# A block-decay attention with two MLPs: a denser opening, other places for the MLP units, and weight loads on ScalarE's DMA queue

## The chip, the cores and the metric

The kernel runs on one core of a Trainium2 chip. The metric is device time in microseconds (us). Before the change three runs gave 595.54 us as their median, from 594.19 to 596.04. Engines are named as the profile names them: PE is TensorE (PEld its weight loads), DVE VectorE, ACT ScalarE, POOL GpSimd, SP SyncE.

## The reference, cut to what matters

Attention with a decay per head over 2 batches, 8 heads, 768 positions, head size 64, and then two MLPs on 1536 tokens of width 512 (inner widths 1536 and 2048), all in float32:

```python
for b in range(nb):                                   # blocks of a sequence
    intra = einsum('bhic,bhjc->bhij', qb, kb) * Dmask # lam ** (i - j), lower triangle
    intra = einsum('bhij,bhjd->bhid', intra, vb)
    inter = einsum('bhid,bhde->bhie', qb * lam_pow, kv_state)
    out[:, :, sl] = intra + inter
    kv_state = lam_block * kv_state + einsum('bhsd,bhse->bhde', kb * rev_pow, vb)
x = out as [tokens, heads * head size]
x = (silu(x @ w_gate) * (x @ w_val)) @ w_out          # first MLP
h = x @ w_in2
y = (h * cos(h)) @ w_out2                             # second MLP
```

## The kernel before

**Stages.** The attention is cut into 12 chunks g of 128 positions (6 per batch). For a chunk PE does: `t` (L1008), four transposes of q and four of k; `s` (L1025), the products of k and q; `st` (L1032), the update of the state from v and the decayed k; `av` (L1038), scores by v; `qs` (L1047), the old state by the decayed q. Between them ACT copies the transposed q and k out of PSUM (tiles qt, kt), DVE multiplies the scores with the decay mask (tile at), POOL makes the decayed k and q (kd, qd) and the decayed state (stmp), and ACT and DVE split the chunk's output into a high and a low part (xh, xl). The MLPs follow: every product is done as three fp32r matmuls of 512 columns (L140 to L142), and DVE and ACT do the activations. A weight piece comes as raw words (512 KB: one DMA of that size, or two of 256 KB for gate and val), goes through ACT (L179), DVE and ACT again, and lies in a ring as a high and a low half (wh, wl).

**Units in the attention.** Some products of the first MLP, 12 matmuls of 512 columns each ("a unit"), can run as soon as four chunks are done and their weights are there. `FILL` says after which chunk's place in the list of steps how many units stand.

**The opening.** `tables()` builds the decay mask: lam goes through a tiny matmul (L238) to all partitions, small copies put it into `powers` and `lrow`, a chain of 14 DVE instructions (L255) builds the skewed table from powers, POOL fills `lrow`, and a step `mask` (L1016) spreads the table by matmuls. In between PE multiplies a tile of zeros (`zero()`, L220), which computes nothing that is used.

**What sets the order.** A planner, run when the program is built, holds a clock per engine and hands out the instructions in the order in which they could start by its own estimates (`ATT_NS`, `free_at`, `LATENCY`, `LANDING`); each engine then runs its own list in order. Where the planner expects PE to stand idle for longer than `ZERO_FROM` before an attention step, it writes in so many zero matmuls (`COLD` or `ZERO` ns each). Every DMA before the change but one stands in SP's list (lam's is in ACT's): q, k and v by `qkv_job` (L870, one DMA of 256 KB each), weights by `load_piece` (L158 to L168). q and k have three buffers each, v five, raw weights three. In the program the DMAs take eight semaphores in turn, so each DMA waits on its queue's engine until the DMA eight before it has landed.

Of the kernel before, what the change touches and what calls it, by code (L numbers as in the profile page):

```python
# [12 lines left out]
AF = mybir.ActivationFunctionType  # L13
# [13 lines left out]
SBUFS = (6, 3)  # L27
UNIT_BANKS = 2, 4
LOOK = 4
ZERO, ZERO_FROM = 230, 300  # L30
COLD, COLD_TO = 430, 6500
KEPT = 4
TAIL = 2
SEQ = 1
# [10 lines left out]
LATENCY = 130  # L45
ISSUE = 620
LANDING = 1900
ATT_NS = {"t": 480, "mask": 700, "s": 1100, "st": 530, "av": 1080, "qs": 600}
FILL = (0, 0, 0, 0, 0, 1, 1, 1, 1, 1, 1, 1)
HELD = 6, 7, 8, 9  # L50
BUFS = {"q": 3, "k": 3, "v": 5, "qt": 2, "kt": 2, "qd": 3, "kd": 2, "at": 2, "stmp": 2}
WARM = 3, 5


FIRST = ("gate", "val", "sa", "sb", "mid")
# [3 lines left out]
def kernel(  # L59
# [19 lines left out]
    nc = tc.nc  # L79
    B, H, S, D = q.shape  # L80
    P = 128
# [3 lines left out]
    C = P  # L85
    NPAIR = H // 2
# [46 lines left out]
    def bank_tile(i):  # L133

        return banks.tile([P, 512], F32, tag=f"bank{i}", name=f"bank{i}")
# [9 lines left out]
    up_w = {"gate": w_gate, "val": w_val, "in2": w_in2}  # L145
    down_w = {"mid": w_mid, "out2": w_out2}

    raw, scaled, fp, wsp = {}, {}, {}, {}

    def load_piece(key, i):  # L150

        nm, f = key
        t = raw[key] = stage_tile(i)
        if nm in ("gate", "val"):


            for c in range(2):
                nc.sync.dma_start(  # L158
                    t[64 * c:64 * c + 64].rearrange("p (k f) -> p k f", k=KD),
                    up_w[nm][256 * c:256 * c + 256, f * 2 * P:(f + 1) * 2 * P].rearrange("(k p) f -> p k f", p=D),  # L160
                )
        elif nm in up_w:
            nc.sync.dma_start(
                t.rearrange("p (c f) -> p c f", c=KD),
                up_w[nm][:, f * 2 * P:(f + 1) * 2 * P].rearrange("(c p) f -> p c f", p=P),
            )
        else:
            nc.sync.dma_start(t, down_w[nm][f * P:(f + 1) * P, :])  # L168

    def word_tile(i):  # L170

# [25 lines left out]
    att = att_stack.enter_context(tc.tile_pool(name="att", bufs=1))  # L197
# [4 lines left out]
    lams = att.tile([1, H], F32, name="lams")  # L202
    ones = att.tile([1, P], F32, name="ones")
    powers = att.tile([P, 7, 2], F32, name="powers")
    anti = att.tile([P, P], F32, name="anti")
    dmask = att.tile([P, H, C], F32, name="dmask")
    zeros = att.tile([P, 512], mybir.dt.bfloat16, name="zeros")
    QB = 32
    skewed = [s_tile(i, f"skewed{i}")[:, 0:2 * (2 * C - QB)].rearrange("p (g y) -> p g y", g=2) for i in range(2)]
    lrow = att.tile([P, NPAIR, C], F32, name="lrow")  # L210
# [6 lines left out]

    def zero(ps, n):
        for _ in range(n):
            nc.tensor.matmul(ps, zeros[:, 0:P], zeros, start=True, stop=True)  # L220

    def tables():

        nc.vector.memset(ones, 1.0)
        nc.scalar.dma_start(lams, lam.rearrange("(o h) -> o h", o=1))
        nc.scalar.activation(warm, halfpi, AF.Silu)
        for t in skewed:
            nc.vector.memset(t, 0.0)  # L230
        for r in range(P // QB):
            nc.vector.tensor_copy(
                skewed[0][QB * r:QB * r + QB, :, C - QB:C],
                anti[QB * r:QB * r + QB, C - QB * (r + 1):C - QB * r].rearrange("p (o y) -> p o y", o=1).to_broadcast([QB, 2, QB]),
            )
        zero(bank_tile(0), WARM[0])
        every = bank_tile(1)[:, 0:H]
        nc.tensor.matmul(every, ones, lams, start=True, stop=True)  # L238
        zero(bank_tile(0), WARM[1])
        for r in range(P // QB):  # L240
            rows = slice(QB * r, QB * r + QB)
            if r % 2:
                nc.scalar.activation(powers[rows, 0, :], every[rows, 2 * r:2 * r + 2], AF.Copy)
            else:
                nc.vector.tensor_copy(powers[rows, 0, :], every[rows, 2 * r:2 * r + 2])
        for h2 in range(2):
            rows = slice(64 * h2, 64 * h2 + 64)
            nc.scalar.activation(lrow[rows, :, C - 1], every[rows, h2::2], AF.Copy)
        for i in range(7):
            m, (src, dst) = 1 << i, (skewed[i % 2], skewed[1 - i % 2])  # L250
            if i:
                nc.gpsimd.tensor_tensor(out=powers[:, i, :], in0=powers[:, i - 1, :], in1=powers[:, i - 1, :], op=ALU.mult)  # L252
            w = max(0, C - QB + 1 - 2 * m)
            for g in range(2):
                nc.vector.scalar_tensor_tensor(  # L255
                    out=dst[:, g, w:C], in0=src[:, g, w + m:C + m], scalar=powers[:, i, g:g + 1], in1=src[:, g, w:C],
                    op0=ALU.mult, op1=ALU.add,
                )
        n = 1
        while n < C:  # L260
            nc.gpsimd.tensor_tensor(
                out=lrow[:, :, C - 2 * n:C - n], in0=lrow[:, :, C - n:C],
                in1=lrow[:, :, C - n:C - n + 1].to_broadcast([P, NPAIR, n]), op=ALU.mult,
            )
            n *= 2
# [5 lines left out]
            xs[nm, blk] = tuple(xp.tile([P, KD, TB], F32R, tag=f"{t}{blk}", name=t) for t in ("xh", "xl"))  # L271
        return xs[nm, blk]

    steps_of = [("t", "q", 0), ("t", "k", 0), ("mask",), ("s", 0), ("t", "q", 1), ("t", "k", 1), ("s", 1)]
    for g in range(NCH):
        if g % CPB != CPB - 1:
            steps_of.append(("st", g))
# [39 lines left out]
    for i in range(0, NF2, GROUP2):  # L317
        p = [[("in2", 2, i + j)] for j in range(4)]
# [20 lines left out]
    def work(op):  # L339

        if op[0] in ATT_NS:
            return ATT_NS[op[0]] / 1360
        if op[0] == "h":
# [93 lines left out]
        **{nm: [(0, i) for i in range(n)] for nm, n in BUFS.items()},  # L437
    }
    wanted = {pool: [] for pool in stock}
    free_at = {"PE": 4100, "ACT": 3300, "DVE": 5900, "POOL": 7300, "SP": 700, "port": 0}  # L440
    waiting = {e: [] for e in ("ACT", "DVE", "POOL", "SP")}
    n_jobs = [0]
    pe_att, pe_units, pe_downs = [], [], []
# [46 lines left out]
    def signal(name, t):  # L490

        when[name] = t
        for job in blocked.pop(name, ()):
            resume(job, t)
# [11 lines left out]
    def go(engine, ns, fn, port=False):  # L506

        return engine, ns, fn, port or engine == "POOL"
# [25 lines left out]
    def run_all():  # L534

        while True:
            best = None
            for e in waiting:
                for job, req in waiting[e]:
                    if not allowed(e, job, req):  # L540
                        continue
                    start = max(free_at[e], job.t, free_at["port"] if req[3] else 0)
                    rank = max(start, free_at[e]), job.prio, job.n
                    if best is None or rank < best[0]:
                        best = rank, e, job, req
            op = next_pe()
            if op and (best is None or op[0] < best[0][0]):
                start, sub = op
                idle = start - free_at["PE"]
                free_at["PE"] = start + sub["ns"]  # L550
                run_pe(sub, free_at["PE"], int(idle // (COLD if start < COLD_TO else ZERO)) if pe_att and idle > ZERO_FROM else 0)
                continue
            if best is None:
                assert not pe_att and not pe_units and not pe_downs and not blocked, (pe_att[:1], pe_units[:1], pe_downs[:1], blocked, wanted)
                return
            (start, _, _), e, job, req = best
            ns = req[1]
            if req[0] == "any":
                ns = ns[e]
                waiting["DVE"].remove((job, req))  # L560
                waiting["POOL"].remove((job, req))
                req[2](e)
            else:
                waiting[e].remove((job, req))
                req[2]()
            free_at[e] = start + ns
            if req[3]:
                free_at["port"] = start + ns
            resume(job, start + ns + LATENCY)
# [58 lines left out]

    def load_job(key):

        i = yield "take", "stage"
        stage_of[key] = i
        yield from fetch(key, i)

    def fetch(key, i):

        yield go("SP", 2300 if key[0] in up_w else 1700, lambda: load_piece(key, i))
        signal(("load", key), (yield "now",) + LANDING)  # L640

    drafts = {}

# [219 lines left out]
    def qkv_job(nm, g):  # L863

        src = {"q": q, "k": k, "v": v}[nm]
        i = yield "take", nm
        t = att_tile(nm, i)
        b, c = divmod(g, CPB)
        made_att[nm, g] = i, t
        yield go("SP", 1200, lambda: nc.sync.dma_start(t, src[b, :, c * C:(c + 1) * C, :].rearrange("h p d -> p h d")))  # L870
        signal((nm, g), (yield "now",) + LANDING)

    def mask_job(got):

# [598 lines left out]
    with tc.manual_schedule():  # L1473
# [5 lines left out]
        )  # L1479
        make_identity(nc, ident)  # L1480
        tables()
        signal("skewed", 5900)
        signal("lrow", 7500)
        pe_att.extend(att_sub(op) for op in steps_of if op)
        pe_units.extend((product_sub if op[0] in ("q", "r", "h") else up_sub)(op) for op in units)
        for op in downs:
# [47 lines left out]
```

## Time and profile before

| what | value |
|---|---|
| median of three runs | 595.54 us (594.19 to 596.04) |
| the profiled execution's own time | 594.82 us |
| its span, first to last instruction | 593.0 us |
| PE busy | 586.6 us (99%) |
| DVE busy | 498.3 us (84%) |
| ACT busy | 356.4 us (60%) |
| POOL busy | 36.1 us (6%), all of it in the first 80 us |

The profile is of one execution. Its span leaves out what lies before the first and after the last instruction (594.82 against 593.0 us). The attention takes the first 79 us, then the MLPs run to the end. The times in timelines are counted from the start of the span; matmuls are pipelined, so what one kind of step costs is read from the start of its first matmul to the start of the next step's.

### The profile page before, as it was taken

Reading aid. Unit: us, or ns where it says so; the run is one execution under the profiler, and the core shown is the slowest. Engines: PE = TensorE matmul, PEld = TensorE weight load, DVE = VectorE, ACT = ScalarE, POOL = GpSimd, SP = SyncE. Lnnn points to the kernel's source line nnn. Section 1 sums busy time; section 2 is a strip of 40 time slices with the busy share of each in tenths; the row PEclk is TensorE's granted clock in tenths of the full one; section 3 lists DMA queues with packets and bytes.
Section 4 is the critical chain, followed back from the end, with each engine's and each line's share of the span. In section 5 each row is a group of like instructions: output and inputs, shape, how many; then the busy total and the mean of one; then the engine's idle time right before and its main releaser. Section 6 shows DMA issues by size and latency. Waiting matters only on the chain.

```text
span 593.0 us, 9131 instructions
## 1 busy us (share of the span) xinstructions
PE 586.6 (99%) x3372; PEld 487.5 (82%) x3372; DVE 498.3 (84%) x922; ACT 356.4 (60%) x664; POOL 36.1 (6%) x50
## 2 busy tenths in 40 slices
PE   9999999999999999999999999999999999999997
PEld 5878788888888888888888888888888888888886
DVE  5669769986699899886899999897797999998854
ACT  3664357685567556545543687977556576676620
POOL 5635200000000000000000000000000000000000
PEclk9999999999999999999999999999999999999999
DMA  9999704264576747524442433011111213100005
GB/s 191 185 204 199 157 30 107 72 202 157 162 225 198 181 141 216 159 82 162 139 161 72 143 106 106 2 55 53 55 35 56 70 54 92 51 1 0 1 6 207
DMA packets 72815, 66.65 MB, mean 112 GB/s; under 512 B 40002, under 2 KB 60738, under 8 KB 72770
## 3 DMA queue, kind: packets, MB, share of 16 engines
q1 hardware_dynamic: 72768, 66.07, 41.2%
q8 instruction: 26, 0.43, 0.3%
q14 instruction: 19, 0.16, 0.1%
q10 hardware_dynamic: 2, 0.00, 0.0%
HBM read 54.00 MB, written 12.06 MB: 111 GB/s over the span
## 4 chain that ended last, share of the span: by engine, by line
PE 97%; DMA 1%; POOL 0%; ACT 0%; issue 0%; DVE 0%
PE bank L140 25%; PE bank L141 24%; PE bank L142 24%; PE bank L1367 6%; PE bank L1368 6%; PE bank L1369 6%; PE bank L1008 2%; PE bank L1025 2%; PE bank L1038 2%; DMA k<-in_k_dram 1%; PE bank L1047 1%; PE bank L1032 1%; PE bank L220 0%; POOL powers L252 0%; PE bank L1016 0%
## 5 line engine op out<-in xcount | busy, mean ns | idle before, releaser
L140 PE MATMUL bank<-xl,wh 128*128 128x512 f32 (+1 forms) x336 | 123.5, 368 | 0.0
L141 PE MATMUL bank<-xh,wh 128*128 128x512 f32 (+1 forms) x336 | 122.5, 365 | 0.0
L142 PE MATMUL bank<-xh,wl 128*128 128x512 f32 (+1 forms) x336 | 122.3, 364 | 0.0
L522 ACT ACTIVATE s<-s 128x512 f32<-128x512 f32 (+2 forms) x112 | 66.0, 592 | 50.5 <-DVE s L515 30.6
L522 ACT ACTIVATE s<-bank 128x512 f32<-128x512 f32 (+2 forms) x114 | 61.1, 538 | 50.2 <-PE bank L142 42.9
L522 ACT ACTIVATE gh<-s 128x512 fp32r<-128x512 f32 x84 | 52.7, 627 | 46.7 <-PE bank L1368 22.3
L140 PE MATMUL bank<-wl,gh 128*128 128x512 f32 (+1 forms) x194 | 75.0, 387 | 0.0
L141 PE MATMUL bank<-wh,gh 128*128 128x512 f32 (+1 forms) x194 | 75.0, 387 | 0.0
L142 PE MATMUL bank<-wh,gl 128*128 128x512 f32 (+1 forms) x194 | 75.0, 387 | 0.0
L140 PEld LDWEIGHTS bank<-xl,wh 128*128 128x128 f32 x336 | 63.3, 188 | 12.0 <-issue 0.7
L515 DVE TENSOR_TENSOR sum<-bank,sum 128x512 f32<-128x512 f32 (+1 forms) x101 | 65.4, 679 | 9.0 <-PE bank L142 7.3
L142 PEld LDWEIGHTS bank<-xh,wl 128*128 128x128 f32 x336 | 63.3, 188 | 10.3
L141 PEld LDWEIGHTS bank<-xh,wh 128*128 128x128 f32 x336 | 63.3, 188 | 10.1
L522 ACT ACTIVATE wh<-ct 128x512 fp32r<-128x512 f32 x91 | 55.3, 627 | 23.5 <-DVE ct L191 14.9
L515 DVE TENSOR_TENSOR gl<-s,gh 128x512 fp32r<-128x512 f32 x84 | 57.5, 685 | 13.7 <-ACT gh L522 13.6
L527 DVE TENSOR_TENSOR wl<-ct,wh 128x512 fp32r<-128x512 f32 x90 | 61.2, 693 | 6.7 <-ACT wh L522 6.5
L515 DVE TENSOR_TENSOR s<-bank,s 128x512 f32<-128x512 f32 (+1 forms) x84 | 49.5, 591 | 11.2 <-PE bank L142 10.6
L1368 PE MATMUL bank<-gh,wh 128*128 128x512 f32 x144 | 56.2, 391 | 0.0
L1367 PE MATMUL bank<-gh,wl 128*128 128x512 f32 x144 | 56.2, 391 | 0.0
L1369 PE MATMUL bank<-gl,wh 128*128 128x512 f32 x144 | 56.0, 389 | 0.0
L179 ACT ACTIVATE ct<-raw 128x512 f32<-128x512 f32 x68 | 44.8, 665 | 14.1 <-DMA raw<-in_moe_w_gate_dram 6.4
L191 DVE SCALAR_TENSOR_TENSOR ct<-ct,raw 128x512 int32<-128x512 int32 x68 | 46.5, 686 | 1.6 <-ACT ct L179 0.7
(145 smaller groups left out, 980.3 us busy)
## 6 DMA issues: line engine op xcount, KB each, us to landing
raw<-in_moe_w_out_dram SPq DMA_DIRECT2D x28, 512.0 KB, 3.5
raw<-in_moe_w_in_dram SPq DMA_DIRECT2D x16, 512.0 KB, 3.9
raw<-in_moe_w_gate_dram SPq DMA_DIRECT2D x24, 256.0 KB, 5.3
raw<-in_moe_w_val_dram SPq DMA_DIRECT2D x24, 256.0 KB, 4.5
draftout<-raw SPq DMA_DIRECT2D x9, 512.0 KB, 2.6
q<-in_q_dram SPq DMA_DIRECT2D x12, 256.0 KB, 5.1
k<-in_k_dram SPq DMA_DIRECT2D x12, 256.0 KB, 5.6
v<-in_v_dram SPq DMA_DIRECT2D x12, 256.0 KB, 6.1
```

The lines of the kernel that those rows point to most:

```text
L140: nc.tensor.matmul(ps, wh, xl, start=first, stop=False, **kw)
L141: nc.tensor.matmul(ps, wh, xh, start=False, stop=False, **kw)
L142: nc.tensor.matmul(ps, wl, xh, start=False, stop=last, **kw)
L179: nc.scalar.activation(t, words[:, :, 1].bitcast(F32), AF.Prelu, scale=2.0 ** -112, alpha=2.0 ** 32)
L191: nc.vector.scalar_tensor_tensor(out=w, in0=w, scalar=3, in1=lo, op0=ALU.logical_shift_left, op1=ALU.bitwise_or)
L515: engine, n * (1.18 if engine == "DVE" else 2.45), lambda: unit.tensor_tensor(out=out, in0=in0, in1=in1, op=op),
L522: return go("ACT", 40 + n * 0.94, lambda: nc.scalar.activation(out, src, fn, **kw))
L527: return "any", {"DVE": n * 1.18, "POOL": n * 2.45}, lambda e: (nc.vector if e == "DVE" else nc.gpsimd).tensor_tensor(out=out, in0=in0, in ...
L1008: nc.tensor.transpose(ps[:, p * P:(p + 1) * P], src[:, 2 * p:2 * p + 2, :].rearrange("p a d -> p (a d)"), anti if op[1] == "q" else ident,)
L1367: nc.tensor.matmul(ps, lo[:, cs], gh, start=first, stop=False)
L1368: nc.tensor.matmul(ps, hi[:, cs], gh, start=False, stop=False)
L1369: nc.tensor.matmul(ps, hi[:, cs], gl, start=False, stop=last)
```

## The change

The zero matmuls have half as many columns (256) and half the price in the planner's eyes. lam's tiny matmul becomes six, which put the values where they are wanted, so that one DVE copy and one ACT copy stand where there were two of DVE and four of ACT. One of two memsets goes from DVE to POOL. In the list of steps the second chunk's `t` stands ahead of the first `s`. `FILL` has six units in place of seven, none before the eighth place. DMAs get one account of what has landed (`landing`). And while attention steps are left, a weight's DMA stands in ACT's list, not SP's.

```diff
-ZERO, ZERO_FROM = 230, 300
-COLD, COLD_TO = 430, 6500
+ZERO, ZERO_FROM = 115, 250
+COLD, COLD_TO = 215, 7500
...
+BEHIND = 7000
+ATT_NS = {"t": 480, "mask": 400, "s": 1100, "st": 530, "av": 1080, "qs": 600}
+FILL = (0, 0, 0, 0, 0, 0, 0, 1, 1, 1, 1, 2)
...
-WARM = 3, 5
+WARM = 4, 5
...
-    def load_piece(key, i):
+    def load_piece(key, i, queue=nc.sync):
...
-                nc.sync.dma_start(
+                queue.dma_start(
                     t[64 * c:64 * c + 64].rearrange("p (k f) -> p k f", k=KD),
...
-            nc.tensor.matmul(ps, zeros[:, 0:P], zeros, start=True, stop=True)
+            nc.tensor.matmul(ps[:, 0:256], zeros[:, 0:P], zeros, start=True, stop=True)
...
-        for t in skewed:
-            nc.vector.memset(t, 0.0)
+        nc.vector.memset(skewed[0], 0.0)
+        nc.gpsimd.memset(skewed[1], 0.0)
...
         zero(bank_tile(0), WARM[0])
-        every = bank_tile(1)[:, 0:H]
-        nc.tensor.matmul(every, ones, lams, start=True, stop=True)
+        every = bank_tile(1)
+        for r in range(P // QB):
+            nc.tensor.matmul(
+                every[QB * r:QB * r + QB, 0:2], ones[:, 0:QB], lams[:, 2 * r:2 * r + 2], start=True, stop=True, tile_position=(0, QB * r)
+            )
+        for h2 in range(2):
+            nc.tensor.matmul(
+                every[64 * h2:64 * h2 + 64, 2:2 + NPAIR], ones[:, 0:64], lams[:, h2::2], start=True, stop=True, tile_position=(0, 64 * h2)
+            )
         zero(bank_tile(0), WARM[1])
...
-                nc.vector.tensor_copy(powers[rows, 0, :], every[rows, 2 * r:2 * r + 2])
...
+        nc.vector.tensor_copy(powers[:, 0, :], every[:, 0:2])
+        nc.scalar.activation(lrow[:, :, C - 1], every[:, 2:2 + NPAIR], AF.Copy)
...
-    steps_of = [("t", "q", 0), ("t", "k", 0), ("mask",), ("s", 0), ("t", "q", 1), ("t", "k", 1), ("s", 1)]
+    steps_of = [("t", "q", 0), ("t", "k", 0), ("mask",), ("t", "q", 1), ("t", "k", 1), ("s", 0), ("s", 1)]
...
-    free_at = {"PE": 4100, "ACT": 3300, "DVE": 5900, "POOL": 7300, "SP": 700, "port": 0}
+    free_at = {"PE": 3850, "ACT": 3300, "DVE": 5700, "POOL": 7200, "SP": 500, "port": 0}
...
+    landed = [2500]
+
+    def landing(soonest, ns):
+
+        landed[0] = max(soonest, landed[0] + ns)
+        free_at["SP"] = max(free_at["SP"], landed[0] - BEHIND)
+        return landed[0] + LATENCY
...
-        yield go("SP", 2300 if key[0] in up_w else 1700, lambda: load_piece(key, i))
-        signal(("load", key), (yield "now",) + LANDING)
+        if pe_att:
+            yield go("SP", 10, lambda: None)
+            yield go("ACT", 1300, lambda: load_piece(key, i, nc.scalar))
+            signal(("load", key), landing((yield "now",) - LATENCY - 1300 + 3600, 2500))
+        else:
+            yield go("SP", 2300 if key[0] in up_w else 1700, lambda: load_piece(key, i))
+            signal(("load", key), (yield "now",) + LANDING)
```

**The opening on PE.** Before, from the last matmul of the first `s` to the second `s` (L1008 is `t`, with anti for q and ident for k; L1025 is `s`):

```order
L1025 MATMUL bank_233<-qt,kt 128x128
L1008 MATMUL bank_247<-anti,q 128x128 x4
L1008 MATMUL bank_258<-ident,k 128x128 x4
L220 LDWEIGHTS zeros
L220 MATMUL bank_272<-zeros 128x512
L220 LDWEIGHTS zeros
L220 MATMUL bank_272<-zeros 128x512
L220 LDWEIGHTS zeros
L220 MATMUL bank_272<-zeros 128x512
L1025 MATMUL bank_272<-qt,kt 128x128
```

In the changed kernel, from the last matmul of the mask (L1030) on (L1022 is `t`, L1039 `s`):

```order
L1030 MATMUL bank_215<-skewed_94,ident 32x256
L1022 MATMUL bank_234<-anti,q 128x128 x4
L1022 MATMUL bank_244<-ident,k 128x128 x4
L1039 MATMUL bank_254<-qt,kt 128x128
L1039 MATMUL bank_255<-qt,kt 128x128
```

The second chunk's transposes come before both `s`, which then follow each other; no zeros stand between them, nor between the first chunk's two transposes, where one stood before.

**The queues.** SP's list before, from the load of the sixth k on:

```order
L870 DMA k<-in_k_dram 128x8x64
L158 DMA raw<-in_moe_w_gate_dram 64x4x256 x2
L870 DMA q<-in_q_dram 128x8x64
L870 DMA v<-in_v_dram 128x8x64
L870 DMA k<-in_k_dram 128x8x64
L158 DMA raw<-in_moe_w_val_dram 64x4x256 x2
```

ACT's list in the changed kernel around the first two weight pieces (L523 are copies, x and xh of a chunk's output):

```order
L159 DMA raw<-in_moe_w_gate_dram 64x4x256 x2
L523 ACTIVATE xh<-bank_535 128x2x128
L523 ACTIVATE xh<-bank_536 128x2x128
L523 ACTIVATE qt<-bank_577 128x512
L523 ACTIVATE kt<-bank_588 128x512
L523 ACTIVATE x_98<-bank_535 128x128
L523 ACTIVATE x_99<-bank_536 128x128
L523 ACTIVATE x_100<-bank_535 128x128
L523 ACTIVATE x_101<-bank_536 128x128
L159 DMA raw<-in_moe_w_val_dram 64x4x256 x2
```

Before, a pair of gate DMAs stood between the sixth and the seventh k (the first and the third L870 k row of the piece above are these two). In the changed kernel the seventh k follows only q and v, and the pair stands in ACT's list, with the copies qt and kt, on which `s` waits, behind it. In all, 16 weight DMAs are in ACT's list, and none is in SP's until the last v has been issued.

**Zeros later in the attention.** In the changed kernel, between the ninth k's transposes and the tenth q's (L221 are zeros):

```order
L1022 MATMUL bank_773<-ident,k 128x128 x4
L221 LDWEIGHTS zeros
L221 MATMUL bank_788<-zeros 128x256
L221 LDWEIGHTS zeros
L221 MATMUL bank_788<-zeros 128x256
L221 LDWEIGHTS zeros
L221 MATMUL bank_788<-zeros 128x256
L221 LDWEIGHTS zeros
L221 MATMUL bank_788<-zeros 128x256
L221 LDWEIGHTS zeros
L221 MATMUL bank_788<-zeros 128x256
L1022 MATMUL bank_788<-anti,q 128x128 x4
```

Five zeros stand here and seven a few steps earlier, ahead of the `st` of the first chunk of the second batch. Before the change two units and no zeros stood in this part of the list; now the first unit comes one `t` and one `s` after these rows.

## Rows read from the trace of the kernel before

**Rows 1.** PE's waits over the span: for whom, us in total, times, longest
```profile
PE bank L1008 <- DMA k<-in_k_dram: 1.4, 1, 1.4
```

**Rows 2.** Busy us (x instructions) by stretch: PE, PEld, DVE, ACT, POOL, PEclk, DMA, GB/s
```profile
20.00:30.00 10.00, 10.00 (x164) 8.34 (x163) 6.86 (x15) 6.20 (x19) 5.53 (x6) 1.00 0.97 186
...
80.00:589.00 509.00, 509.00 (x2439) 427.26 (x2438) 444.01 (x795) 316.91 (x565) 0.00 (x0) 1.00 0.33 101
```

**Rows 3.** Timeline of the stall: start, us, engine, line, what, [idle before <-releaser]
```profile
30.06 0.69 PE L1032 MATMUL bank<-v,kd 128*64 128x64 f32 x16
32.14 0.63 PE L1008 MATMUL bank<-ident,k 128*128 128x128 f32 x4 [1.39 <-DMA k<-in_k_dram]
```

**Rows 4.** Timeline of the opening, PE
```profile
1.19 1.46 PE L220 MATMUL bank<-zeros 128*128 128x512 bf16 x3 [1.19 <-DVE halfpi L1475]
2.58 0.59 PE L238 MATMUL bank<-lams,ones 1*128 1x8 f32 x2
3.10 2.31 PE L220 MATMUL bank<-zeros 128*128 128x512 bf16 x5
5.52 1.09 PE L1008 MATMUL bank<-anti,q 128*128 128x128 f32 x4
6.40 0.63 PE L220 MATMUL bank<-zeros 128*128 128x512 bf16 x1
6.83 1.06 PE L1008 MATMUL bank<-ident,k 128*128 128x128 f32 x4
7.82 1.16 PE L1016 MATMUL bank<-skewed,ident 32*32 32x256 f32 x32
8.90 1.35 PE L1025 MATMUL bank<-qt,kt 64*128 64x128 f32 x16
10.18 0.66 PE L1008 MATMUL bank<-anti,q 128*128 128x128 f32 x4
10.68 0.60 PE L1008 MATMUL bank<-ident,k 128*128 128x128 f32 x4
11.12 0.81 PE L220 MATMUL bank<-zeros 128*128 128x512 bf16 x3
12.02 1.16 PE L1025 MATMUL bank<-qt,kt 64*128 64x128 f32 x16
13.11 0.69 PE L1032 MATMUL bank<-v,kd 128*64 128x64 f32 x16
```

**Rows 5.** DMA from issue to landing: first q, second k, seventh k
```profile
DMA to landing us min/median/max: 3.4/3.4/3.4
...
DMA to landing us min/median/max: 4.9/4.9/4.9
...
DMA to landing us min/median/max: 7.9/7.9/7.9
```

**Rows 6.** Timeline of DMA issues (ACTq, SPq) and of the DVE chain
```profile
0.73 0.51 ACTq L227 DMA_DIRECT2D lams<-in_lam_dram  x1
0.74 0.43 SPq L870 DMA_DIRECT2D q<-in_q_dram  x1
2.86 0.93 SPq L870 DMA_DIRECT2D k<-in_k_dram  x1
3.97 2.92 DVE L255 SCALAR_TENSOR_TENSOR skewed<-skewed,powers 128x33 f32<-128x33 f32 x14 [0.23 <-ACT powers L243]
...
19.57 1.67 SPq L158 DMA_DIRECT2D raw<-in_moe_w_gate_dram  x2
24.12 3.10 SPq L870 DMA_DIRECT2D k<-in_k_dram  x1
...
69.77 1.27 SPq L158 DMA_DIRECT2D raw<-in_moe_w_gate_dram  x2
```

**Rows 7.** Groups on ACT from 13 to 40 us: shapes, count, busy, mean ns, idle
```profile
L522 ACT ACTIVATE qt<-bank 128x512 f32<-128x512 f32 x5 | 3.0, 609 | 0.3 <-PE bank L1008 0.3
```

More of the change, by code (lines that the diff above doesn't have):

```diff
@@ L47 @@
 LANDING = 1900
-ATT_NS = {"t": 480, "mask": 700, "s": 1100, "st": 530, "av": 1080, "qs": 600}
-FILL = (0, 0, 0, 0, 0, 1, 1, 1, 1, 1, 1, 1)
+BEHIND = 7000
+ATT_NS = {"t": 480, "mask": 400, "s": 1100, "st": 530, "av": 1080, "qs": 600}
+FILL = (0, 0, 0, 0, 0, 0, 0, 1, 1, 1, 1, 2)
 HELD = 6, 7, 8, 9
 BUFS = {"q": 3, "k": 3, "v": 5, "qt": 2, "kt": 2, "qd": 3, "kd": 2, "at": 2, "stmp": 2}
-WARM = 3, 5
+WARM = 4, 5
 FIRST = ("gate", "val", "sa", "sb", "mid")
@@ L162, in load_piece @@
         elif nm in up_w:
-            nc.sync.dma_start(
+            queue.dma_start(
                 t.rearrange("p (c f) -> p c f", c=KD),
@@ L167, in load_piece @@
         else:
-            nc.sync.dma_start(t, down_w[nm][f * P:(f + 1) * P, :])
+            queue.dma_start(t, down_w[nm][f * P:(f + 1) * P, :])
     def word_tile(i):
@@ L206 @@
     dmask = att.tile([P, H, C], F32, name="dmask")
-    zeros = att.tile([P, 512], mybir.dt.bfloat16, name="zeros")
+    zeros = att.tile([P, 256], mybir.dt.bfloat16, name="zeros")
     QB = 32
@@ L236, in tables @@
         zero(bank_tile(0), WARM[0])
-        every = bank_tile(1)[:, 0:H]
-        nc.tensor.matmul(every, ones, lams, start=True, stop=True)
-        zero(bank_tile(0), WARM[1])
[L240 to L244, printed above, removed]
-                nc.vector.tensor_copy(powers[rows, 0, :], every[rows, 2 * r:2 * r + 2])
-        for h2 in range(2):
-            rows = slice(64 * h2, 64 * h2 + 64)
-            nc.scalar.activation(lrow[rows, :, C - 1], every[rows, h2::2], AF.Copy)
+        every = bank_tile(1)
[7 more added lines that the diff above has]
+            )
+        zero(bank_tile(0), WARM[1])
+        nc.vector.tensor_copy(powers[:, 0, :], every[:, 0:2])
+        nc.scalar.activation(lrow[:, :, C - 1], every[:, 2:2 + NPAIR], AF.Copy)
         for i in range(7):
@@ L549, in run_all @@
                 idle = start - free_at["PE"]
-                free_at["PE"] = start + sub["ns"]
+                free_at["PE"] = start + sub["ns"] * (2 if start < COLD_TO else 1)
                 run_pe(sub, free_at["PE"], int(idle // (COLD if start < COLD_TO else ZERO)) if pe_att and idle > ZERO_FROM else 0)
@@ L869, in qkv_job @@
         made_att[nm, g] = i, t
-        yield go("SP", 1200, lambda: nc.sync.dma_start(t, src[b, :, c * C:(c + 1) * C, :].rearrange("h p d -> p h d")))
-        signal((nm, g), (yield "now",) + LANDING)
+        yield go("SP", 1100, lambda: nc.sync.dma_start(t, src[b, :, c * C:(c + 1) * C, :].rearrange("h p d -> p h d")))
+        signal((nm, g), landing((yield "now",) - LATENCY - 1100 + 3000, 1200 if landed[0] < 12000 else 1350))
     def mask_job(got):
@@ L1481 @@
         tables()
-        signal("skewed", 5900)
-        signal("lrow", 7500)
+        signal("skewed", 5750)
+        signal("lrow", 7250)
         pe_att.extend(att_sub(op) for op in steps_of if op)
```

## The prediction, made before the result was known

> **What bounds the kernel now.** I read the page's table of engines first, then PE's waits, PE's busy time by stretch, and the timelines of the two places where PE is not full: the opening and about 31 us. From 80 us to 589 us PE is busy for 509.00 of 509.00 us [rows 2], and its list of waits over the whole span has one entry of any size, 1.4 us on a k [rows 1]. So the end is PE's work plus what PE loses in its first 80 us. The change leaves the number of useful matmuls as it is (only lam's, six for one, are more), and the last ones stand in the same order. What it can move is the opening, the one wait, and the zeros. Of the page: DVE is 84% busy, so a wait for DVE later on is possible, but before the change there is none.
>
> The sum is made against the profiled execution (594.82 us, span 593.0); the median of the three runs is 0.7 above it. I carry the difference over to the median. Runs of this kernel differ by up to 1.9 us, and about 0.3% (1.8 us) is what a measurement tells from no change.
>
> **The opening, before.** Steps cost, start to start [rows 4]: a zero of 512 columns 0.43 (6.40 to 6.83), `t` of one tensor 0.88 (5.52 to 6.40) and later 0.50 (10.18 to 10.68), the mask 1.08, the first `s` 1.28, the second 1.09. So TensorE runs at its lower level (1.2 GHz) up to the first `s` and at the upper (2.4 GHz) behind it; PE had been busy nearly without a break since 1.19 us. The first `t` starts at 5.52, behind five zeros that began at 3.10 and lasted 2.31, though its q landed at 0.74 + 3.4 = 4.1 [rows 5, 6]. The second `s` ends at 13.11.
>
> **The opening, after, step by step.**
> - Zeros ahead of lam: four of half width, 4 x 0.21 for 3 x 0.43, 0.4 us less (half of 0.43 for half of the columns is an estimate).
> - lam: 2 passes took 0.52 (2.58 to 3.10); now 12. The mask's 32 passes, which also go to small places of the array, took 1.08, or 0.03 each; at 0.26 each, as before, 12 would be 3.1, at the mask's pitch 0.4. Nearer to the mask, as these too have tile positions: I take 1.0, 0.5 more.
> - Zeros behind lam: 5 x 0.21 for 5 x 0.43: 1.1 us less. So the first `t` starts at 5.52 - 0.4 + 0.5 - 1.1 = 4.5 (not before 4.1, the landing), and the zero of 0.43 behind it is gone: the second `t` starts at 5.4 and ends at 6.3.
> - The mask then waits for the DVE chain, before 3.97 to 6.89 [rows 6]. It began after copies that alternated between DVE and ACT; with one copy, lam ready about as before, it begins some 0.5 earlier and ends at 6.4. Mask 6.4 to 7.5 (before 7.82 to 8.90).
> - The second chunk's two `t`, 0.9 each, to 9.3. They need the second k, landed at 2.86 + 4.9 = 7.8; it is there in time. kt of that chunk is copied by ACT, as qt in 0.61 [rows 7], beside the first `s`.
> - Two `s` at 1.09: to 11.5, if the clock rises by then as it did before. The three zeros of 0.81 that filled the wait for kt are gone.
> Gain 13.1 - 11.5 = 1.6 us. Bounds: if the clock rises only behind both `s`, these take twice as long (+2.2): a loss of 0.6. If it rises before the second chunk's `t`, those take 0.5 each and the k's landing sets them: 7.8 + 0.5 + 2.2 = 10.5, a gain of 2.6.
>
> **The wait at 31 us.** PE waits 1.39 us for the seventh k at 32.14 [rows 3]. That k was issued at 24.12, the issue took 3.10 and it landed 7.9 us after its start, 32.0, behind a gate pair issued at 19.57 [rows 5, 6]. The pair now comes after it. The pair's own issue takes 1.67, and it has as many bytes as two k's: the k should land two landings earlier, about 30. PE asks for it at 30.7 less the opening's gain, about 29. Of 1.39 us I count 1.2 as gained, and what is late next is again data: under a faster PE the stream of q, k and v is hardly ahead. Bounds: 0 and 1.4.
>
> **The new zeros.** Twelve of 256 columns at the upper clock: half of a fast 512-column zero. Three of those span 0.81 with the last one's pipeline in it [rows 4]; at half of the cold 0.43 a wide one is 0.21, a narrow one 0.11. 12 x 0.11 = 1.3 us of PE for nothing useful, unless PE would have waited there: then they cost nothing. They stand before an `st` that needs a v and a kd, and before a q. Bounds 0 to 1.3 of loss; I take 1.0.
>
> **Units.** One unit fewer inside the attention is one more behind it, the same twelve matmuls: nothing, covered by nothing and needing no cover, as PE is busy either way.
>
> **ACT's new work.** 16 DMAs to issue. SP took 0.64 for each of a pair when nothing was queued (1.27 for two) and 0.84 when much was (1.67) [rows 6]. A pair thus holds ACT for 1.3 to 1.7 us. ACT is busy for 6.20 of 10 us at 20 to 30 us [rows 2], so 3.8 are free. A pair comes about once a chunk; twelve chunks with their seven units take 79 us, 6.6 each, and one without a unit some 5, in which 1.9 us are free: it fits, with 0.2 to 0.6 to spare. Behind a pair in ACT's list stand xh, qt and kt, and `s` waits for the last two; and each DMA of a pair waits until the DMA eight earlier has landed, in a stream where the seventh k took 7.9 us. That is near. I put 0.4 us of PE waits here; bounds 0 and, with a whole issue of 3.10 in front of each DMA, 2 x 3.7 = 7.4 a pair, 5.5 more than is free.
>
> **Sum.** -1.6 - 1.2 + 1.0 + 0.4 = -1.4 us: 593.4 against the profiled 594.82, or 594.1 at the level of the median. That is 0.24% and inside of what can be told from no change.
>
> **Rivals.**
> 1. More is gained: the clock is up before the second chunk's `t`, the wait is gone and the new zeros stand where PE would have waited: -2.6 - 1.4 + 0.2 = -3.8 at most; with half of the zeros real waits and the opening at -2.2, -2.9: 592.6. For it: nothing but useful work now stands between the first chunk and the second `s`, 1.2 us of zeros less. Against: lam's passes and the clock.
> 2. The stream gives it all back. The first `st` of the second batch then waits for its v as long as PE came earlier: the q, k, v and weights are the same bytes on the same DMA engines, and in 20 to 30 us their share is 0.97 already [rows 2]. Then only the wait's place changes: 0 to -0.4, 595.3. Against: no weights now stand before the seventh k, and after the wait at 31 us PE never waited for a DMA again.
> The Trainium skill ("DMA: Bandwidth & Descriptors", section "Issuing engines are not separate DMA queues") has a rule for this one: a DMA runs on the same 16 engines whichever engine issues it, and issuing from several saves only the issuing time. By it the second queue gives no bandwidth and the sum would be this rival's 595.3. No row here has two full queues at once, so the trace does not decide.
> 3. Slower: ACT is held by its DMA issues. While SP's list is pushing a transfer into a full queue (3.10 for the k), ACT's issue stands still, and with it qt and kt. A first sign: the tiny load of lam, issued by ACT at 0.73, took 0.51 and ended when SP's issue of 0.43 at 0.74 had [rows 6]. If each ACT issue waits out an ordinary one of 1.0, a pair takes 3.3 and overshoots the 1.9 that are free by 1.4; if a long one, by 5.5. Two pairs come while SP is still busy and no unit covers PE: +2.8 to +11; taken +4.5, 598.2. It decides from 1.9 us a pair on. Against it: by the time of the third pair SP is nearly done with q, k and v.
> The Trainium skill ("Perfetto Trace Analysis", section "DMA Instruction — HWDGE (DVE, Sync)") states that the block which writes descriptors is locked by one sequencer at a time. By that rule this rival would hold; the one overlap at 0.73 agrees with it, and no row shows it under load.
>
> **How the numbers follow.** Forecast 0.50 (own range 593.2 to 595.0), more gained 0.22, given back 0.16, slower 0.12. Below 593.75 (faster by over 0.3%) lie a third of the forecast's case and nearly all of the first rival's: 0.38. Above 597.3 lies most of the third's: 0.10. Between them 0.52. The range leaves out the lower half of the first rival and most of the third: 592.4 to 596.4.
>
> **What would show it.** Right: the second `s` ends near 11.5; the first `t` at 4.5; no wait for k near 30; twelve zeros of 0.11 with no wait just behind them; weight issues on ACT of 0.6 to 0.9 each. Wrong: `t` at 0.88 beyond 10 us or an `s` of 2 us (the clock later); waits of PE on ACT's kt or qt behind a weight issue, or issues on ACT of over 1 us (rival 3); a wait of PE on v or q behind the zeros (rival 2); any wait of PE after 80 us.

## The result: slower by 1.2%

The changed kernel took 602.70 us (median of five runs, 598.71 to 603.98), the kernel before 595.06 beside it: ratio 1.0121 [1.0095, 1.0147]. Forecast was 594.1, with a range to 596.4. The profiled execution is the shortest of the five (598.71 us, span 596.9), so the profile shows the loss at its smallest.

PE's list of waits for the changed kernel (for whom, us in total, times, longest), to be held against [rows 1]:
```profile
PE bank L1022 <- DMA k<-in_k_dram: 2.7, 2, 2.3
PE bank L1039 <- ACT kt L523: 1.3, 1, 1.3
...
PE bank L1022 <- DMA q<-in_q_dram: 0.4, 1, 0.4
```
One wait of 1.4 us on a k has become 3.1 us on q and k, and 1.3 on kt. The stretches say where (columns as in [rows 2]; the last row is the whole time behind the attention):
```profile
28.00:32.00 4.00, 4.00 (x76) 3.37 (x68) 2.22 (x5) 2.40 (x8) 0.51 (x1) 1.00 1.18 210
32.00:36.00 4.00, 1.30 (x23) 0.88 (x22) 2.44 (x6) 1.15 (x3) 0.03 (x1) 0.94 1.16 201
36.00:40.00 4.00, 4.00 (x40) 3.06 (x40) 0.49 (x2) 1.30 (x4) 2.25 (x2) 0.63 1.28 198
...
80.00:590.00 510.00, 509.89 (x2451) 428.04 (x2450) 445.85 (x793) 319.23 (x569) 0.00 (x0) 1.00 0.33 100
```
From 32 to 36 us PE works 1.30 of 4 us, and in the next four it is busy at a granted clock of 0.63. From 80 us on next to nothing is lost (0.11 us). PE's timeline there:
```profile
33.02 0.63 PE L1022 MATMUL bank<-anti,q 128*128 128x128 f32 x4 [0.39 <-DMA q<-in_q_dram]
35.95 1.09 PE L1022 MATMUL bank<-ident,k 128*128 128x128 f32 x4 [2.31 <-DMA k<-in_k_dram]
36.96 1.98 PE L1052 MATMUL bank<-at,v 128*64 128x128 f32 x16
...
41.16 0.94 PE L221 MATMUL bank<-zeros 128*128 128x256 bf16 x7
42.03 0.69 PE L1046 MATMUL bank<-v,kd 128*64 128x64 f32 x16
42.54 1.05 PE L1052 MATMUL bank<-at,v 128*64 128x128 f32 x16
```
The eighth k is late, and behind that pause an `av` takes 1.98 us instead of 1.05: TensorE is at its lower level (1.2 GHz). The seven zeros later on have no wait behind them.

The opening, against [rows 4]:
```profile
2.09 0.28 PE L240 MATMUL bank<-lams,ones 1*32 1x2 f32 x8
2.30 0.38 PE L244 MATMUL bank<-lams,ones 1*64 1x4 f32 x4
2.61 1.25 PE L221 MATMUL bank<-zeros 128*128 128x256 bf16 x5
4.35 1.08 PE L1022 MATMUL bank<-anti,q 128*128 128x128 f32 x4 [0.49 <-POOL powers L253]
...
7.66 0.91 PE L1022 MATMUL bank<-anti,q 128*128 128x128 f32 x4
...
8.93 2.25 PE L1039 MATMUL bank<-qt,kt 64*128 64x128 f32 x32
11.11 0.66 PE L1022 MATMUL bank<-anti,q 128*128 128x128 f32 x4
```
The second `s` ends at 11.11; before it ended at 13.11. The opening gained 2.0 us, and more than that was lost between 16 and 54 us. For this execution the account closes: -2.0 of the opening, +3.0 of waits (4.4 on q, k and kt for 1.4), +1.5 of half clock (0.37 of the 4 us from 36 to 40) and +1.4 of the twelve zeros (0.87 and 0.55, start to start) make the 3.9 us by which its span is longer than before.

### The profile page after: what moved, and what is told of

It reads as the page before. It is cut to its first block, busy times and chain, and to the rows that moved or that the text cites. A ratio compares the mean times of both kernels' runs of the same rounds, so it can differ in the third digit from the quotient of the medians.

```text
span 596.9 us, 9166 instructions
## 1 busy us (share of the span) xinstructions
PE 587.6 (98%) x3391; PEld 489.8 (82%) x3391; DVE 500.9 (84%) x921; ACT 356.1 (60%) x661; POOL 33.6 (6%) x50
## 4 chain that ended last, share of the span: by engine, by line
PE 90%; DMA 5%; DVE 2%; ACT 1%; POOL 1%; issue 1%; SPq 0%; ACTq 0%; DVEq 0%; POOLq 0%
PE bank L141 23%; PE bank L142 23%; PE bank L143 23%; PE bank L1381 5%; PE bank L1382 5%; PE bank L1383 5%; DMA k<-in_k_dram 3%; PE bank L1022 2%; PE bank L1052 1%; DMA q<-in_q_dram 1%; DMA raw<-in_moe_w_gate_dram 1%; PE bank L1039 1%; PE bank L1061 1%; DVE s L516 1%; DVE ct L192 1%
## 5 line engine op out<-in xcount | busy, mean ns | idle before, releaser
L523 ACT ACTIVATE s<-bank 128x512 f32<-128x512 f32 (+2 forms) x114 | 61.1, 538 | 52.1 <-PE bank L143 47.2
L523 ACT ACTIVATE gh<-s 128x512 fp32r<-128x512 f32 x84 | 52.9, 631 | 58.2 <-PE bank L1382 31.2
L523 ACT ACTIVATE s<-s 128x512 f32<-128x512 f32 (+2 forms) x112 | 65.5, 589 | 30.8 <-DVE s L516 19.2
L523 ACT ACTIVATE wh<-ct 128x512 fp32r<-128x512 f32 x91 | 55.6, 627 | 28.0 <-DVE ct L192 20.6
```

What stands on the lines that cost most here:

```text
L523: return go("ACT", 40 + n * 0.94, lambda: nc.scalar.activation(out, src, fn, **kw))
```

## The experiments

Theory A: the second queue does the harm. It has two ways: A1, weights on ScalarE's queue pass q, k and v on the transfer engines; A2, ScalarE is held by its weight issues, and kt and qt behind them. Theory B: the units, which now stand later, no longer cover the stream. Theory C: the zeros. In the diffs `-` and `+` are against the changed kernel unless another is named. Every ratio is to the kernel before, run beside it. Some expectations count from 0: the "sixth k" of two of them is the seventh k of the front, and "k of the seventh chunk" is the eighth k here.

**The queue undone.**
```
-            yield go("ACT", 1300, lambda: load_piece(key, i, nc.scalar))
+            yield go("ACT", 1300, lambda: load_piece(key, i))
```


> The changed kernel with one thing undone: the weights of the attention are issued by SyncE, at the same place of the program's order, so that q, k, v and weights come in one row; TensorE's order stays the same to the instruction. Theory A (the second queue: from 26 to 42 us the weights on ScalarE's queue take more than half of the transfer engines, q and k of the seventh chunk come late, TensorE waits 2.7 us on them, the clock goes to half for 3.4 us and a weight issue that stands on ScalarE holds kt for 1.3 us): none of the three is seen, k of the seventh chunk lands by 31 us instead of 35.8, and the time is 592 to 594.5, below before. Theory B (the later units: no MLP unit stands before the eighth chunk, so TensorE runs into data whatever queue brings it): a wait on q or k of 2 us or more stays between 30 and 40 us, the clock still falls there, and the time is 599 to 603. Theory C (the twelve new zero multiplies and the shorter opening's own costs): no data wait, but 598 or more.

594.81 us, ratio 0.9995 [0.9979, 1.0010]: the whole loss is gone, as A said, though the time lies just above A's range (592 to 594.5). PE's waits on data:
```profile
PE bank L1022 <- DMA k<-in_k_dram: 0.8, 1, 0.8
PE bank L1022 <- DMA q<-in_q_dram: 0.4, 1, 0.4
```
How the eighth k came late is seen in the two queues. The profile's rows of DMA queues from 26 to 40 us (packets, MB, share of 16 engines), the changed kernel's first, then this one's:
```profile
DMA packets 8192, 2.89 MB, mean 206 GB/s; under 512 B 7164, under 2 KB 8188, under 8 KB 8188
...
q1 hardware_dynamic: 7101, 1.79, 77.6%
q10 hardware_dynamic: 1087, 1.05, 39.0%
```
```profile
DMA packets 7915, 2.74 MB, mean 196 GB/s; under 512 B 6992, under 2 KB 7911, under 8 KB 7911
...
q1 hardware_dynamic: 7911, 2.69, 99.4%
```
The sum is nearly the same, 206 and 196 GB/s: a second queue (q10, ScalarE's) brought no bandwidth worth the name. What differs is the order. The first gate pair and the eighth k as they were issued, with two queues and then with one:
```profile
25.64 0.74 ACTq L159 DMA_DIRECT2D raw<-in_moe_w_gate_dram  x1
...
26.03 0.99 SPq L884 DMA_DIRECT2D k<-in_k_dram  x1
26.43 0.62 ACTq L159 DMA_DIRECT2D raw<-in_moe_w_gate_dram  x1
```
```profile
25.54 0.98 SPq L884 DMA_DIRECT2D k<-in_k_dram  x1
...
27.69 3.11 SPq L159 DMA_DIRECT2D raw<-in_moe_w_gate_dram  x2
```
With one queue the pair stands behind that k; with two it goes beside it, and the weights take their part (39.0% against the 77.6% of SyncE's queue; not more than half, as the expectation has it) while the k is on its way. From issue to landing the eighth k took 9.8 us with two queues and 6.2 us with one:
```profile
DMA to landing us min/median/max: 9.8/9.8/9.8
```
```profile
DMA to landing us min/median/max: 6.2/6.2/6.2
```

**The units put back.**
```
-FILL = (0, 0, 0, 0, 0, 0, 0, 1, 1, 1, 1, 2)
+FILL = (0, 0, 0, 0, 0, 1, 1, 1, 1, 1, 1, 1)
```


> The changed kernel with the units put back to where they stood before (one in each chunk from the sixth on); the weights stay on ScalarE's queue. Theory A (second queue): q, k and v still come late while weights are under way, and the unit in the sixth chunk now waits for its weights too: 598 to 603. Theory B (later units): the unit at 34 to 37 us covers the seventh k, no wait over 1 us on it, the clock stays up, 592.5 to 595. Theory C (zeros): 598 or more without data waits.

599.83 us, 1.0079 [1.0057, 1.0102]. The time is in A's range. It is 2.9 us below the changed kernel, and the two intervals just overlap: an early unit seems to cover a part of what the queue does. In this run's profiled execution (597.86 us, the shortest of six) PE waits for no data longer than 0.5 us and the granted clock is 1.00, as B said; it waits for kt three times, 1.8 us in all.

**The queue alone, in the kernel before.**
```
-        yield go("SP", 2300 if key[0] in up_w else 1700, lambda: load_piece(key, i))
+        yield go("SP", 2300 if key[0] in up_w else 1700, lambda: load_piece(key, i, nc.scalar if pe_att else nc.sync))
```


> The kernel before with one part of the change alone: weights taken in the attention are issued by ScalarE, with before's opening, units and planner account. Theory A (second queue): q/k/v fall to some 40% of the engines while weights are under way, TensorE waits 2 us or more between 28 and 42 us, with or without a clock at half: 597 to 602, slower than before. Theory B (later units): the units are where they were, so 594 to 596, as before; the 1.4 us wait at 32 us on the sixth k may even go, since weights no longer stand ahead of it in SyncE's row (593.7).

601.63 us, 1.0109 [1.0087, 1.0130]: this one part makes nearly all of the change's loss. But PE's waits are mostly not on data, as A1 had it, but on ScalarE. PE's list, and then ScalarE's own from 20 to 80 us:
```profile
PE bank L1025 <- ACT kt L522: 2.7, 3, 1.5
PE bank L1038 <- ACT qt L522: 1.9, 1, 1.9
PE bank L1008 <- DMA k<-in_k_dram: 1.4, 1, 1.4
```
```profile
ACT ct L179 <- DMA raw<-in_moe_w_val_dram: 9.2, 3, 3.8
...
ACT ct L179 <- DMA raw<-in_moe_w_gate_dram: 5.8, 3, 3.6
```
Here ScalarE is held less by the issues than by the conversion of weights that land late (3.9 and 4.1 us in the kernel before), with qt and kt behind it in its list. The weights are also issued later: the second gate pair at 40.79 us, before at 36.11.

**The opening alone, in the kernel before** (its diff is that of the change without the queue, `FILL`, `BEHIND` and `landing`).

> The kernel before with the opening of the change alone (multiplies of 256 zeros, the lam products, the order of the first steps, the planner's opening numbers); queue, units and the account of loads are those of before. The second s ends near 11 us instead of 13.1. What follows is the question: in before TensorE waited 1.4 us at 32 us on the sixth k, which landed at 32.0 behind weights. If the data sets the time there (theory B's side: TensorE is ahead of the transfers), the wait grows to 3 to 3.4 us, nothing is left of the 2 us, the clock may fall to half behind it, and the time is 594.5 to 597. If the opening's gain stays (theory A: only the second queue did harm) it is 592.8 to 593.6.

595.69 us, 1.0011 [0.9999, 1.0022]. The gain of 2 us is all given back, though in several waits and not in the one of 3 us:
```profile
PE bank L1008 <- DMA k<-in_k_dram: 2.5, 2, 1.5
...
PE bank L1032 <- DMA v<-in_v_dram: 0.8, 1, 0.8
```
PE comes earlier to data that do not. With its weights ahead of the seventh k in SyncE's row, the kernel before is at the stream's pace up to that point.

**The weights on GpSimd's queue** (`nc.scalar` to `nc.gpsimd` in `fetch`).

> The changed kernel with the weights of the attention issued by GpSimd instead of ScalarE: still a second queue beside SyncE's, at the same places of the program, but ScalarE, which makes qt and kt, issues none. The queue costs by two ways that this tells apart. Theory A1 (the transfer engines are shared: a second queue passes the line of q, k and v): q and k of the seventh chunk land late as in the changed kernel (k at 34 us or later against 31.7 where SyncE issued the weights), TensorE waits 2 us or more on them, 598 to 603. Theory A2 (ScalarE is held: an issue waits for the transfer eight earlier, and kt and qt wait behind it): no wait on kt, and 594 to 596.5.

597.00 us, 1.0030 [1.0014, 1.0046]. Between the two ranges: by the ratios (1.0121, 1.0030, 0.9995) 5.4 us of the loss go with ScalarE's part and 2.1 stay. GpSimd's queue differs in more than the engine (it moved the 1.05 MB in 320 packets, not 1087, and in the program its transfers take turns with none of SyncE's), so this alone does not settle A2. What stays looks like A1. The profiled execution (598.91 us, the longest of twelve) has a wait of 2.2 us on a q, though not on the k, and behind it `qs` and a part of `s` at half speed:
```profile
37.05 1.09 PE L1022 MATMUL bank<-anti,q 128*128 128x128 f32 x4 [2.19 <-DMA q<-in_q_dram]
38.07 1.13 PE L1061 MATMUL bank<-qd,state 64*64 64x128 f32 x16
39.13 1.70 PE L1039 MATMUL bank<-qt,kt 64*128 64x128 f32 x16
```

**The queue undone and the units put back.**

> The changed kernel with SyncE issuing the weights and the units where they stood before (one in each chunk from the sixth). What the later units are worth by themselves, beside the run that had only the queue undone (594.81). Theory A: the first weights are wanted at 36 us, so they stand ahead of the sixth k in SyncE's row as in before, and TensorE, 2 us earlier, waits 1.5 to 3 us there: 595 to 597. Theory B (an early unit covers the stream): no wait over 1 us between 20 and 45 us: 593 to 594.3.

595.09 us, 0.9991 [0.9976, 1.0006]; no wait on data over 0.5 us, so A's reason was wrong here and B's right, though the time is A's. With one queue the units' place cannot be told (594.81 and 595.09).

**No zeros in the attention,** with SyncE issuing the weights, and with ScalarE:
```
-                run_pe(sub, free_at["PE"], int(idle // (COLD if start < COLD_TO else ZERO)) if pe_att and idle > ZERO_FROM else 0)
+                run_pe(sub, free_at["PE"], int(idle // COLD) if pe_att and idle > ZERO_FROM and start < COLD_TO else 0)
```


> The changed kernel with SyncE issuing the weights and without the twelve zero multiplies inside the attention (those of the opening stay). With the zeros it was 594.81, and its trace shows 0.87 and 0.55 us of them with no wait of TensorE behind them. Theory C (the zeros cost their time): 593.3 to 593.9. If they only fill time in which data is on its way: the wait on k at 16 us stays at 0.8, a wait of 0.5 to 1.4 us comes up at 37 to 42 us, 594.3 to 595.2.

594.57 us, 0.9986 [0.9969, 1.0003]: of the zeros' 1.4 us a new wait of 0.7 us on v has taken half; 0.2 us less in all is nothing that can be told.

> The changed kernel, weights on ScalarE's queue, without the twelve zero multiplies inside the attention. Theory C (the zeros are a part of the loss): 601.0 to 601.6, by 1.1 to 1.4 less than the changed kernel's 602.7. Theory A (data sets the time there): TensorE comes sooner to the same late data and waits longer, 602 to 604.

602.07 us, 1.0109 [1.0082, 1.0135]. Theory C falls as the cause of the loss. What the zeros cost is not settled: 0.6 us less than 602.70 is well inside the two intervals, and so would be the 1.1 to 1.4 that C asked for. The waits now show more of ScalarE:
```profile
PE bank L1039 <- ACT kt L523: 4.1, 1, 4.1
PE bank L1022 <- DMA k<-in_k_dram: 2.3, 3, 1.0
PE bank L1022 <- DMA q<-in_q_dram: 1.9, 2, 0.9
```

**Tiny transfers on ScalarE,** weights on SyncE:
```
...
+            nc.scalar.dma_start(lams[:, n:n + 1], lam[n:n + 1].rearrange("(o h) -> o h", o=1))
```


> SyncE issues the weights, as in the run that had only the queue undone (594.81), and ScalarE issues, at the places where the changed kernel had its weight transfers, as many transfers of one number each (four bytes, from lam, used by nothing). They take next to nothing of the transfer engines, but an issue on ScalarE still waits its turn for the transfer eight earlier. Theory A2 (it is this holding of ScalarE that costs most of the queue's 7 us): waits on kt or qt of 2 us or more between 30 and 75 us, 598 to 602. Theory A1 (only the weights' bytes on a second queue harm): no such wait, 594.5 to 596.

594.69 us, 0.9988 [0.9971, 1.0005]. A2 as I had put it fell, but the try was weak. The issues took 0.2 to 0.3 us each, and the longest that one stood was from 31.2 to 32.5 us, until the transfer eight earlier had landed; the others stood less or not at all. It shows that issuing on ScalarE costs nothing that can be told by itself, and not what a long stand costs.

**Four buffers for k; and the planner's account corrected as well** (both without zeros, weights on SyncE):
```
-BUFS = {"q": 3, "k": 3, ...
+BUFS = {"q": 3, "k": 4, ...
...
-            yield go("SP", 10, lambda: None)
-            yield go("ACT", 1300, lambda: load_piece(key, i, nc.scalar))
+            yield go("SP", 2300 if key[0] in up_w else 1700, lambda: load_piece(key, i))
```


> SyncE issues the weights, no zero multiplies in the attention (594.57 so far), and four buffers for k instead of three, which puts the fourth k ahead of the fifth q in SyncE's row. The wait of 0.7 us on that k at 17 us goes; if nothing takes its place, 593.6 to 594.1 and a ratio to before that leaves 1 out; if the data behind it come later by as much, 594.4 to 595.

594.58 us, 0.9989 [0.9975, 1.0004]: nothing gained. The wait on that k did not go: PE still waits 0.7 us, now at 16.34.

> As the last, and the planner's account tells the truth again on who issues the weights (SyncE's time is charged, none of ScalarE's): the row on SyncE takes the weights as their account says, somewhat later among q, k and v, and ScalarE's copies are placed without 1.3 us set aside for each weight. If the account mattered: 592.5 to 593.8. If only the queue did: within 0.4 us of the run with four k buffers.

593.93 us, 0.9977 [0.9961, 0.9993]: by 0.23% the one version here that beats both kernels, less than expected; its interval just leaves 1 out, and from the run with four k buffers it cannot be told. No wait on q, k or v over 0.5 us is left; GpSimd's kd (1.2) and kt (0.7) are late instead:
```profile
PE bank L1045 <- POOL kd L516: 1.2, 1, 1.2
...
PE bank L1038 <- ACT kt L523: 0.7, 1, 0.7
```

**kt and qt taken from behind ScalarE's issues** (no zeros, weights on ScalarE, from the chunk g = 8 on):
```
-        yield act(t.rearrange("p a i -> p (a i)"), ps, AF.Copy)
+        if g >= 8:
+            yield go("ACT", 520, lambda: nc.vector.tensor_copy(t.rearrange("p a i -> p (a i)"), ps))
+        else:
+            yield act(t.rearrange("p a i -> p (a i)"), ps, AF.Copy)
```


> The changed kernel without the zeros in the attention (602.07 so far; its trace has one wait of 4.1 us on kt at 54 us, behind a weight issue that stood on ScalarE, and 4.2 us of waits on q and k), and with the copies of q and k from the eighth chunk on (counted from 0) made by VectorE instead of ScalarE. Theory A2 (what stands on ScalarE behind the weight issues costs): the 4.1 us wait goes, 598 to 599.5. Theory A1 (the late q and k alone): 601.5 to 603, TensorE waiting elsewhere.

597.52 us, 1.0033 [1.0015, 1.0051]: 4.5 us less than with the copies on ScalarE, though VectorE got more work. So what holds kt and qt in ScalarE's list is most of the loss, as A2 said. The edit takes them from behind all that stands there, issues and conversions alike. VectorE's copies with the weights on SyncE were not tried; in that kernel without the zeros (594.57) PE's list has no wait for kt or qt that they could take away.

**The first two pieces on the other engine than the rest** (no zeros):
```
-            yield go("ACT", 1300, lambda: load_piece(key, i, nc.scalar))
+            yield go("ACT", 1300, lambda: load_piece(key, i, nc.sync if key in loads[:2] else nc.scalar))
```
and, in the second run,
```
-            yield go("ACT", 1300, lambda: load_piece(key, i, nc.scalar))
+            yield go("ACT", 1300, lambda: load_piece(key, i, nc.scalar if key in loads[:2] else nc.sync))
```


> The changed kernel without the zeros in the attention, the first two pieces of weights (gate and val of the first unit pair) on SyncE, all later ones on ScalarE. Theory A1 says where the first pair's share of the loss lies: no q or k wait over 1 us between 30 and 42 us and the clock stays up there; what the second pair does at 47 to 56 us (kt held, 2 to 4 us) stays: 597.5 to 600. If the first pair alone did the harm: 594 to 595.5. If the later ones alone: 601 or more.

> The complement: the first two pieces on ScalarE's queue, all later ones on SyncE, no zeros in the attention. Waits on q and k of 2 to 4 us and half a clock between 32 and 42 us stay, no kt wait at 54 us: 597.5 to 600. If the first pair alone did the harm: 601 or more; if the later ones alone: 594 to 595.5. With the run before it the two losses over the 594.6 of SyncE for all should come to about the 7.5 us of ScalarE for all (602.07), if they add.

600.01 us, 1.0092 [1.0055, 1.0128], with the later pieces on ScalarE, and 598.03 us, 1.0038 [1.0016, 1.0060], with the first two there; 597.5 to 600 was forecast for either. Against 0.9986 with all on SyncE these lose 6.3 and 3.1 us; together 9.4, where all on ScalarE lost 7.3: both do harm, the later ones more, and they don't quite add. The first of the two shows the holding in the open. ScalarE's timeline (ACTq is its DMA issues), then PE's:
```profile
45.49 0.60 ACT L523 ACTIVATE s<-bank 128x512 f32<-128x512 f32 x1 [1.15 <-PE bank L143]
45.55 0.60 ACTq L159 DMA_DIRECT2D raw<-in_moe_w_val_dram  x1
45.98 0.62 ACT L523 ACTIVATE wh<-ct 128x512 fp32r<-128x512 f32 x1
50.78 0.60 ACTq L159 DMA_DIRECT2D raw<-in_moe_w_val_dram  x1
51.43 0.60 ACT L523 ACTIVATE kt<-bank 128x512 f32<-128x512 f32 x1 [4.83 <-DMA k<-in_k_dram]
```
```profile
48.06 0.66 PE L1022 MATMUL bank<-anti,q 128*128 128x128 f32 x4
52.08 2.08 PE L1039 MATMUL bank<-qt,kt 64*128 64x128 f32 x16 [3.37 <-ACT kt L523]
54.09 1.12 PE L1022 MATMUL bank<-ident,k 128*128 128x128 f32 x4
```
The second half of a val piece stands at the head of ScalarE's list until 50.78, when a k landed (issued at 42.25, 8.5 us earlier), the DMA eight before it in the program; the copy of kt behind it waits 4.83 us, PE 3.37, and PE then runs an `s` in 2.08 us, for 1.16 at the upper clock.

## Why the prediction was wrong, by its steps

- The opening, -1.6: right, -2.0. lam's twelve passes took 0.52 us (2.09 to 2.61), half of the estimate.
- The wait at 31 us, -1.2: it went, but the step stopped at "what is late next is again data" and gave that no price. The next data, q and k of the eighth chunk, cost 0.4 and 2.3 us, and the clock behind them 1.5 more. The opening's run shows what this step and the first have in common: a faster PE in front of a stream at its limit gains nothing (595.69). With the queue undone, too, the steps other than ACT's do not give their sum: -1.8 us by the prediction, -0.3 measured (-1.25 to +0.6).
- The new zeros, +1.0: their size was right (1.4 us in all, 1.3 expected), their cost could not be told (0.2 us with one queue, 0.6 with two). With one queue half of their time came back as a wait on v.
- The units, 0, "covered by nothing and needing no cover": right for one queue (594.81 and 595.09), probably wrong for two (602.70 and 599.83), where an early unit seems to cover a part of the loss.
- **ACT's new work, +0.4: the step that failed.** It had the right wait, on the DMA eight earlier, "in a stream where the seventh k took 7.9 us", and then sized it by ScalarE's spare time. An issue that stands is not work that fits into gaps: it holds whatever is behind it until that DMA has landed. The runs put the holding of kt and qt at 4.5 us (copies on VectorE; 5.4 with GpSimd's queue). And the sum had no term for weights that pass q, k and v: some 2 to 3 us by the same runs.
- Rival 2 (595.3) is what the runs with one queue gave: 594.81, and 595.69 for the opening alone. For two queues it had the shared engines and nothing of the size. By its rule in the Trainium skill ("DMA: Bandwidth & Descriptors", section "Issuing engines are not separate DMA queues") a second issuing engine gives no bandwidth; the trace agrees, 206 GB/s with two queues and 196 with one. The cost came from the order: the second queue took its part at once, from loads that PE was about to wait for.
- Rival 3 named the engine, the price (+4.5) and the side, with a chance of 0.12, and the wrong cause; that its price is also what the holding cost is luck. Of its signs, the waits on kt behind a weight issue came true, issues on ACT of over 1 us did not. The rule it leaned on in the Trainium skill ("Perfetto Trace Analysis", section "DMA Instruction — HWDGE (DVE, Sync)") says that one sequencer at a time writes descriptors. In the changed kernel an ACT issue took its 0.60 us inside one of SyncE's that took 4.24, so no lock for the whole of an issue is seen:
```profile
48.67 4.24 SPq L884 DMA_DIRECT2D v<-in_v_dram  x1
...
49.31 0.60 ACTq L159 DMA_DIRECT2D raw<-in_moe_w_val_dram  x1
```
The wait lay ahead of the issue, on a landing, not in it.

Open: the other four runs of the changed kernel have spans 2.7 to 5.1 us longer than the profiled one, at mean granted clocks from 0.991 to 0.997. Three of them are lower than the profiled one's 0.997 and so spent more time at the lower clock; where, and what the rest waited for, is not shown, as only the one execution has a profile. The nearest is the changed kernel without the later zeros, profiled at 602.07 us: its kt wait is 4.1 us for 1.3, and from 50 to 60 us its granted clock is 0.83.

## What to carry to other kernels

Before a transfer is moved to another queue, ask which transfers it will pass: here, with the engines at their limit, one queue in order of need beat two. Where DMAs take semaphores in turn, as here, a DMA issue on an engine that also computes can be a wait in that engine's list for a transfer to land, and is priced by that landing and by what stands behind the issue, not by the 0.6 us that it takes. And a gain ahead of a stage that goes at the pace of its data is no gain until the data come earlier too.

## Not expected

A pause of PE of 2.31 us (data) or 3.37 us (kt) was followed by work at half clock: `av` in 1.98 us for 1.05, `s` in 2.08 for 1.16. The slower work behind the first cost 1.5 us more than the list of waits says. The 1.39 us of [rows 3] had no such row behind it.
